# Eight raw weight buffers, a re-spaced split schedule and earlier token gathers in an attention + routed experts + FFN kernel

## The chip, the cores and the metric

The kernel runs on one core of one Trainium2 chip. The metric is the device time of one execution in microseconds (us); the number compared is the median of several executions. TensorE (PE) multiplies and transposes, VectorE (DVE) and ScalarE (ACT) do elementwise work, GpSimd (POOL) issues indirect gathers, and SyncE (SP) issues most DMAs.

## The reference

Three stages run one after the other on 1536 tokens of width 512, all in float32.

1. Chunked local attention with 8 memory keys per head; its output is x[1536, 512].
2. A routed layer with 8 experts: `expert = argmax(x @ w_gate)`, a softmax weight for the chosen expert, at most 384 tokens per expert, then `relu(x_e @ w1[e]) @ w2[e]` with w1[e] 512x1024 and w2[e] 1024x512.
3. A dense layer: `h = x @ w_in` (512x2048), `g = max(0.01 h, h)`, `g @ w_out` (2048x512). Its two weight matrices arrive as 64-bit floats.

```python
h = np.maximum(np.einsum('ecd,edf->ecf', disp, w1), 0.0)
y = np.einsum('ecf,efd->ecd', h, w2)
...
h = x @ w_in
g = np.maximum(0.01 * h, h)
return (g @ w_out).astype(np.float32)
```

## The kernel before

**Weights.** Every matmul is done as three fp32r matmuls on high and low parts (high times low, high times high, low times high), so each weight tile has to be split. A 512 KB piece (an item) is loaded by SP into a raw buffer (tile `raw`, `load_ahead`, L178 to L187); ACT casts its high part into a ring slot (L221) and DVE subtracts for the low part (L225). The subtraction frees the raw buffer, and only then SP may issue the next load: at most `RAWS` = 5 items are loaded or waiting. An expert has eight items (A0, B0, A1, B1 of two items each; A is w1, B is w2). The ring has eight slots, four per expert, and a slot is free once the expert two earlier has used it (`RETIRE`, `slot_free`).

The FFN's weights have 32 items of 64-bit floats. Their conversion, `wide_stages` (L122 to L148), has three stages: ACT writes a square into a scratch tile `c` and rescales the low word (L132, L133); DVE does six operations (L137 to L145); ACT and DVE split the result (L119, L120). An item passes one stage at a call, then the next one a call later, and the split two calls after that.

**Order.** The order of work on each engine is the program's order. `feed(n)` advances the weight generator by n items at hand-set places: after each of the six phases of an expert (`FEED_FIRST` for expert 0, `FEED_MID` for 1 to 5, `FEED_NEXT`, `FEED_LAST`), and after some steps of the FFN (`FEED_FFN`). `enter(e + 1)` at the end of expert e feeds what is still missing of the next expert's weights. Counted along this order, the items split at the ends of experts 0 to 5 are 20, 29, 38, 46, 54 and 62.

**An expert** (`expert`, L676 to L762). If it has more than 256 tokens, a third block of 128 rows is done first (`block`, under the `If` of L684): transposes (L771), `xc` split by ACT and DVE (L773, L774), 24 matmuls (L787), then relu, transposes and 24 more (L805). Then come six phases. Above 128 tokens, phases 0 to 3 compute hidden units (L694) and phases 2 to 5 the rows (L701); with 1 to 128 tokens the 24 matmuls of L706 fill phases 0 and 1, transposes (L711) phases 2 and 3, and L715 phases 4 and 5; with none, TensorE only fills (L719). After each of phases 0 to 3, ACT and DVE write the split hidden values `hs` (L742, L746) and for phases 0 and 1 a plain copy `t` (L745). Inside the phases named by `NEXT_AT`, the next expert's tokens are transposed on TensorE (L660, into the single PSUM buffer `tp`) and split by ACT and DVE into `xsT` (L662, L663). At the end DVE copies y[0] and ACT y[1] to `o` (L760), and SP stores them.

In this input the experts differ: 0, 5 and 6 have up to 128 tokens, 1 has up to 256, 2, 3 and 7 have the third block, 4 has no tokens.

**Gathers.** POOL gathers 128 token rows at a time into one of five `nat` buffers (L640), three per expert (`gathers`, nested in `experts`), issued in program order at the start of the expert before.

Of the kernel before, what the change touches and what calls it, by code (L numbers as in the profile page):

```python
# [6 lines left out]
F32 = mybir.dt.float32  # L7
# [11 lines left out]
P = 128  # L19
# [10 lines left out]
NEG = -1e30  # L30
RING = 8
NQ = 4
RAWS = 5
FLIGHT = 3
SHARE = (0,)
GAP_FEED = 2
# [1 line left out]
DRAIN_FEED = ((0, 0), (1, 0), (1, 0), (0, 0))  # L38
ROUTE_STEPS = 5
ROUTE_FEED = ((15, 0), (19, 0), (20, 0))  # L40
FEED_FIRST = (2, 1, 1, 3, 2, 3)
FEED_MID = (2, 0, 0, 3, 2, 2)
FEED_NEXT = (2, 0, 0, 1, 1, 0)
FEED_LAST = (1, 1, 1, 1, 0, 0)
FEED_GAP = 2
RETIRE = (None, ("A", 0), None, ("A", 1), ("B", 0), ("B", 1))
FEED_FFN = (0, 2, 3, 4, 6, 7, 8, 10, 11)
NEXT_AT = (2, 3)
MIN_HIGH = 2.0 ** -15 * 1.125


class Builder:
# [69 lines left out]
    def wide_stages(self, raw, dst, eng):  # L122
        nc, dv = self.nc, self.nc.vector
        w = raw.rearrange("p (n w) -> p n w", w=2)
        lo_w, lo_f, hi_f = w[:, :, 0], w[:, :, 0].bitcast(F32), w[:, :, 1].bitcast(F32)

        def buf(tag):
            return self.mp.tile([P, 512], U32, name=tag, tag=tag, bufs=3)

        c = [buf("c0")]  # L130
        cf = [c[0].bitcast(F32)]
        nc.scalar.activation(out=cf[0], in_=hi_f, func=AF.Square)  # L132
        nc.scalar.activation(out=lo_f, in_=lo_w, func=AF.Copy, scale=2.0 ** -52)  # L133
        yield
        c.append(buf("c1"))
        cf.append(c[1].bitcast(F32))
        dv.scalar_tensor_tensor(out=cf[0], in0=cf[0], scalar=MIN_HIGH * MIN_HIGH, in1=hi_f,  # L137
                                op0=ALU.is_ge, op1=ALU.mult)
        dv.tensor_scalar(out=c[1], in0=c[0], scalar1=3, scalar2=0x3FFFFFFF,  # L139
                         op0=ALU.logical_shift_left, op1=ALU.bitwise_and)  # L140
        dv.scalar_tensor_tensor(out=c[1], in0=c[0], scalar=0xC0000000, in1=c[1],  # L141
                                op0=ALU.bitwise_and, op1=ALU.bitwise_or)
        dv.tensor_scalar(out=c[0], in0=c[1], scalar1=0xFF800000, scalar2=None, op0=ALU.bitwise_and)  # L143
        dv.tensor_tensor(out=cf[0], in0=lo_f, in1=cf[0], op=ALU.mult)  # L144
        dv.tensor_tensor(out=cf[1], in0=cf[1], in1=cf[0], op=ALU.add)  # L145
        self.held -= 1
        yield
        self.split_piece(cf[1], dst, eng)  # L148

# [26 lines left out]
        return src[m * P:(m + 2) * P].rearrange("(k p) f -> p k f", p=P)  # L176

    def load_ahead(self):  # L178
        while self.held < RAWS:
            nxt = next(self.rawgen, None)  # L180
            if nxt is None:
                return
            raw = self.spool.tile([P, 1024], F32 if nxt[1] < E else U32, name="raw", tag="raw", bufs=RAWS)
            self.nc.sync.dma_start(out=raw.rearrange("p (k f) -> p k f", k=2) if nxt[1] < E else raw,
                                   in_=self.weight_source(*nxt))
            self.raws.append(raw)
            self.held += 1  # L187

    def weights_gen(self):
        flying, count = [], 0  # L190

        def advance():
            for rec in list(flying):
                rec[1] += 1
                if rec[1] == 1 or rec[1] == rec[2]:
                    next(rec[0], None)
                    if rec[1] > 1:
                        flying.remove(rec)
                        self.ready.add(rec[3])

        for kind, e, i, m in self.items:
            self.load_ahead()
            if m == 0:
                while e == E and i > self.quarter or (kind, e, i) not in self.W and not self.slot_free():
                    advance()
                    yield
                self.weight_slot((kind, e, i))
            raw, dst = self.raws.pop(0), self.W[(kind, e, i)]
            if e == E:
                advance()  # L210
                st = self.wide_stages(raw, (dst[:, 0, m, :], dst[:, 1, m, :]),
                                      self.nc.vector)
                next(st)
                flying.append([st, 0, self.flight, (kind, e, i, m)])
                yield
                continue
            advance()
            count += 1
            raw = raw.rearrange("p (k f) -> p k f", k=2)
            hi, lo = dst[:, 0, m:m + 2, :], dst[:, 1, m:m + 2, :]  # L220
            self.nc.scalar.copy(out=hi, in_=raw)  # L221
            mode = self.share[count % len(self.share)]
            for j, n in ((0, 2),) if mode == 0 else ((0, 1), (1, 1)):
                eng = self.nc.gpsimd if (mode == 2 or mode == 1 and j) else self.nc.vector
                eng.tensor_tensor(out=lo[:, j:j + n], in0=raw[:, j:j + n], in1=hi[:, j:j + n].bitcast(F32),  # L225
                                  op=ALU.subtract)
            self.ready |= {(kind, e, i, m), (kind, e, i, m + 1)}
            self.held -= 1
            self.load_ahead()
            yield  # L230
        while flying:
            advance()
            yield
# [293 lines left out]
    def prologue(self):  # L527
        nc = self.nc
        with ExitStack() as ctx:
# [46 lines left out]
            ones_cols(self.vb[2])  # L576
            self.load_qk(3)
            NU = 2 * NI
            self.W, self.ready, self.raws, self.held, self.items = {}, set(), [], 0, self.weight_items()
            self.rawgen = iter(self.items)  # L580
            self.wgen = self.weights_gen()
            self.flight, self.share, self.quarter = FLIGHT, SHARE, 0
            for u in range(NU + 4):
# [54 lines left out]
    def gather(self, idx, col, src):  # L638
# [2 lines left out]
                                          in_offset=bass.IndirectOffsetOnAxis(ap=idx[:, col:col + 1], axis=0))  # L641
        return t

    def clear_rows(self, e):
        for j in range(2, self.nj):
            r0 = e * self.slots + j * P
            self.nc.sync.dma_start(out=self.ys[r0:r0 + P, :].rearrange("p (r d) -> p r d", d=P),
                                   in_=self.zero.unsqueeze(1).to_broadcast([P, DM // P, P]))
# [27 lines left out]
    def expert(self, e):  # L676
        nc, nj = self.nc, self.nj
        xs = self.xsT.pop(e)
        feeds = {0: FEED_FIRST, E - 2: FEED_NEXT, E - 1: FEED_LAST}.get(e, FEED_MID)
        pcnt = self.pcnts.pop(e)  # L680
        if nj > 2:
            cnt, nat = self.cnts.pop(e), self.natx.pop(e, [])
# [44 lines left out]
        for ph, (many, few) in enumerate(phases):  # L727
            if ph < 4:
                hps[ph] = self.mps.tile([P, 512], F32, name="h", tag="h", bufs=3)
            with self.tc.If(pcnt > P) as cmp:  # L730
                many()
            with cmp.Else():
                if ph == 5:
                    fill(y[1])
                with self.tc.If(pcnt > 0) as some:
                    few()
                with some.Else():
                    if ph != 4:
                        fill(hps[ph] if ph < 4 else y[0])
            if ph < 4:  # L740
                h = hs[ph] = self.mp.tile([P, 2, 512], F32R, name="hs", tag="hg", bufs=4)
                nc.scalar.activation(out=h[:, 0, :], in_=hps[ph], func=AF.Relu)  # L742
                if ph < 2:
                    ts[ph] = self.mp.tile([P, 512], F32, name="t", tag="hg", bufs=4)
                    nc.scalar.activation(out=ts[ph], in_=hps[ph], func=AF.Relu)  # L745
                nc.vector.scalar_tensor_tensor(out=h[:, 1, :], in0=hps[ph], scalar=0.0,  # L746
                                               in1=h[:, 0, :].bitcast(F32), op0=ALU.max, op1=ALU.subtract)
            self.retired |= {RETIRE[ph] and (RETIRE[ph][0], e, RETIRE[ph][1])}
            if e + 1 < E:
                if ph == 0:  # L750
                    self.clear_rows(e + 1)
                    self.counts(e + 1)
                if ph in NEXT_AT:
                    self.expert_x(e + 1, NEXT_AT.index(ph))
            self.feed(feeds[ph])
        if e + 1 < E:
            self.enter(e + 1)
        for j in range(2):
            o = self.npool.tile([P, DM], F32, name="o", tag="o", bufs=2)
            (nc.scalar.copy if j else nc.vector.tensor_copy)(out=o, in_=y[j])  # L760
            r0 = e * self.slots + j * P
            (nc.scalar if e == E - 1 and j else nc.sync).dma_start(out=self.ys[r0:r0 + P, :], in_=o)  # L762

    def block(self, e, j, nat):
        nc = self.nc
# [56 lines left out]
    def experts(self):  # L822
        nc = self.nc
        self.nat, self.natx, self.xsT, self.cnts, self.pcnts = {}, {}, {}, {}, {}

        def gathers(e):
            self.nat[e] = [self.gather(self.tab, e * self.nj + j, self.xs) for j in range(2)]
            self.natx[e] = [self.gather(self.tab, e * self.nj + 2, self.xs)] if self.nj == 3 else []

        gathers(0)  # L830
        self.feed(GAP_FEED)
        self.keep_warm(self.mps.tile([P, 512], F32, name="tp", tag="acc", bufs=4), WARM[1])
        self.expert_x(0, 0)
        self.expert_x(0, 1, "acc", 4)
        self.enter(0)
        self.counts(0)
        for e in range(E):
            if e + 1 < E:
                gathers(e + 1)
            self.expert(e)  # L840


# [112 lines left out]
    def build(self):  # L955
# [11 lines left out]
        self.prologue()  # L967
        with ExitStack() as c2:
            self.mp = self.npool = self.pool(c2, "moe")
            self.mps = self.pool(c2, "mps", space=PSUM)  # L970
            self.experts()
            self.ffn()
# [35 lines left out]
```

## Time and profile before

| what | value |
|---|---|
| runs (us) | 623.01 (median), 623.58, 619.49 |
| profiled execution | 626.9 us, span 625.1 us |
| TensorE busy | 548.3 us (88% of the span) |
| VectorE busy | 408.2 us (65%) |
| ScalarE busy | 300.4 us (48%) |
| mean granted TensorE clock | 0.945 of full speed |

The span runs from the first to the last instruction of the profiled execution; the execution's time is 1.8 us longer. In the rows below times are us from the start of the span. Attention and routing take the first 96 us, the experts 96 to 330, the FFN the rest. A row of a timeline is a run of like instructions on one engine; what stands in brackets is the idle time just before it and what ended it.

### The profile page before, as it was taken

The numbers are of one execution on the slowest core, as the hardware profiler recorded it, in microseconds if no ns is written. First come the engines' busy times: TensorE is split into PE (matmuls) and PEld (weight loads), VectorE is DVE, ScalarE is ACT, GpSimd is POOL, SyncE is SP. The second block draws the span as 40 slices with busy tenths as digits, with TensorE's granted clock in tenths as the row PEclk, the third lists the DMA queues.
The fourth block names the chain that finished last, engine by engine and source line by source line (L and its number), as shares of the span: only waits on it lengthen the run. The fifth ranks groups of instructions, "written<-read, shape, count | busy, mean of one in ns | idle before, by whom it ended". The sixth has DMA issues, their size and how long they took to land.

```text
span 625.1 us, 9434 instructions
## 1 busy us (share of the span) xinstructions
PE 548.3 (88%) x3393; PEld 446.0 (71%) x3393; DVE 408.2 (65%) x672; ACT 300.4 (48%) x520; POOL 69.0 (11%) x104
## 2 busy tenths in 40 slices
PE   7799946796996993688997899999999999999997
PEld 6566635685895982466886778788887788777886
DVE  4776776836136347676298687874888878885443
ACT  7999646635135346465243455545344344432211
POOL 7323242101001012000004110000000000000000
PEclk9999967789898996698999999999999999999999
DMA  7899949966328139975136331310222211000111
GB/s 187 188 213 195 283 145 333 332 213 220 134 70 288 66 103 331 297 225 221 60 100 222 100 118 35 100 50 21 68 68 67 69 57 44 1 1 0 68 67 68
DMA packets 66857, 84.80 MB, mean 136 GB/s; under 512 B 22768, under 2 KB 39408, under 8 KB 66800
## 3 DMA queue, kind: packets, MB, share of 16 engines
q1 hardware_dynamic: 61456, 68.95, 36.5%
q0 software_dynamic: 3904, 12.59, 6.7%
q10 hardware_dynamic: 1440, 2.49, 1.1%
q8 instruction: 38, 0.62, 0.4%
q14 instruction: 19, 0.16, 0.1%
HBM read 70.64 MB, written 13.37 MB: 134 GB/s over the span
## 4 chain that ended last, share of the span: by engine, by line
DVE 25%; PE 23%; ACT 5%; issue 3%; DMA 1%; DVEq 0%; ACTq 0%; POOL 0%; POOLq 0%
PE acc L914 9%; PE h L893 9%; DVE t L902 3%; DVE gt L904 3%; ACT gt L903 3%; DVE c L144 3%; DVE c L141 3%; DVE c L137 2%; DVE ring L120 2%; DVE c L139 2%; DVE c L143 2%; DVE c L145 1%; PE h L706 1%; DVE total L930 1%; PE acc L715 1%
## 5 line engine op out<-in xcount | busy, mean ns | idle before, releaser
L893 PE MATMUL h<-x,ring 128*128 128x512 f32 (+1 forms) x600 | 141.8, 386 | 3.1 <-ACT x L878 2.7
L914 PE MATMUL acc<-ring,gt 128*128 128x512 f32 x576 | 138.7, 390 | 4.6 <-DVE rest L930 2.9
L914 PEld LDWEIGHTS acc<-ring,gt 128*128 128x128 f32 x576 | 107.7, 188 | 28.9 <-ACT t L901 5.0
L893 PEld LDWEIGHTS h<-x,ring 128*128 128x128 f32 x600 | 110.1, 191 | 25.3 <-ACT x L878 3.6
L225 DVE TENSOR_TENSOR ring<-raw,ring 128x1024 fp32r<-128x1024 f32 x64 | 75.5, 1223 | 15.6 <-ACT ring L221 14.6
L903 ACT CAST gt<-t 128x512 fp32r<-128x512 f32 x48 | 29.8, 621 | 96.1 <-DVE t L902 96.1
L221 ACT CAST ring<-raw 128x1024 fp32r<-128x1024 f32 x64 | 63.9, 1052 | 17.6 <-DMA raw<-in_moe_w_dram 17.6
L901 ACT COPY t<-h 128x512 f32<-128x512 f32 x48 | 28.2, 587 | 63.2 <-PE h L893 63.1
L902 DVE SCALAR_TENSOR_TENSOR t<-h,t 128x512 f32<-128x512 f32 x48 | 32.9, 685 | 35.4 <-ACT t L901 35.4
L904 DVE TENSOR_TENSOR gt<-t,gt 128x512 fp32r<-128x512 f32 x48 | 33.3, 693 | 33.0 <-ACT gt L903 33.0
L746 DVE SCALAR_TENSOR_TENSOR hs<-h,hs 128x512 fp32r<-128x512 f32 x32 | 21.7, 687 | 49.6 <-ACT hs L742 26.9
L694 PE MATMUL h<-xsT,ring 128*128 128x256 f32 x384 | 49.4, 289 | 3.7 <-issue 3.1
L694 PEld LDWEIGHTS h<-xsT,ring 128*128 128x128 f32 x384 | 48.4, 197 | 4.6 <-issue 4.3
L742 ACT ACTIVATE hs<-h 128x512 fp32r<-128x512 f32 x32 | 19.5, 608 | 58.7 <-PE acc L701 34.8
L701 PE MATMUL acc<-ring,hs 128*128 128x512 f32 x192 | 46.0, 392 | 0.0
L640 POOL DMA_INDIRECT nat<-xs,tab x24 | 24.1, 1006 | 159.5 <-PE tp L660 137.9
L701 PEld LDWEIGHTS acc<-ring,hs 128*128 128x128 f32 x192 | 35.3, 188 | 7.0
L787 PE MATMUL h<-ring,xc 128*128 128x512 f32 x72 | 22.4, 470 | 11.0 <-ACT xc L773 11.0
L706 PE MATMUL h<-ring,xsT 128*128 128x512 f32 x72 | 24.3, 509 | 8.3 <-DVEq L684 5.5
L706 PEld LDWEIGHTS h<-ring,xsT 128*128 128x128 f32 x72 | 18.0, 257 | 14.5 <-issue 7.5
L787 PEld LDWEIGHTS h<-ring,xc 128*128 128x128 f32 x72 | 16.2, 233 | 15.3 <-ACT xc L773 11.7
L144 DVE TENSOR_TENSOR c<-raw,c 128x512 f32<-128x512 f32 x32 | 22.2, 693 | 1.2
(162 smaller groups left out, 739.1 us busy)
## 6 DMA issues: line engine op xcount, KB each, us to landing
raw<-in_moe_w_dram SPq DMA_DIRECT2D x64, 512.0 KB, 5.6
raw<-in_moe_w_in_dram SPq DMA_DIRECT2D x16, 512.0 KB, 3.8
raw<-in_moe_w_out_dram SPq DMA_DIRECT2D x16, 512.0 KB, 3.4
ys<-o SPq DMA_DIRECT2D x15, 256.0 KB, 6.0
kn<-in_k_dram SPq DMA_DIRECT2D x16, 192.0 KB, 2.7
qn<-in_q_dram SPq DMA_DIRECT2D x16, 192.0 KB, 4.1
xs<-x POOLq DMA_DIRECT2D x16, 192.0 KB, 4.6
vb<-in_v_dram SPq DMA_DIRECT2D x12, 176.0 KB
```

What stands on the lines that cost most here:

```text
L144: dv.tensor_tensor(out=cf[0], in0=lo_f, in1=cf[0], op=ALU.mult)
L221: self.nc.scalar.copy(out=hi, in_=raw)
L225: eng.tensor_tensor(out=lo[:, j:j + n], in0=raw[:, j:j + n], in1=hi[:, j:j + n].bitcast(F32), op=ALU.subtract)
L694: nc.tensor.matmul(hps[f // 2][:, f % 2 * 256:f % 2 * 256 + 256], w["A", f // 4][:, wi, k, c], xs[xi][:, k, :], start=(n == 0), stop=(n == ...
L701: nc.tensor.matmul(y[j], hs[f // 2][:, hi, c:c + P], w["B", f // 4][:, wi, f % 4, :], start=(f == 0 and n == 0), stop=(f == 7 and n == 2))
L706: nc.tensor.matmul(hps[i], xs[xi][:, k, :P], w["A", i][:, wi, k, :], start=(n == 0), stop=(n == 11))
L787: nc.tensor.matmul(hp[i], xc[:, xi, k, :], w[:, wi, k, :], start=(n == 0), stop=(n == 11))
L893: nc.tensor.matmul(hps[s][:, t], w[:, wi, k, c], X[g][:, xi, k, t], start=(n == 0), stop=(n == 11))
L902: nc.vector.scalar_tensor_tensor(out=t, in0=hp, scalar=0.01, in1=t, op0=ALU.mult, op1=ALU.max)
L903: nc.scalar.copy(out=gt[:, 0, :], in_=t)
L904: nc.vector.tensor_tensor(out=gt[:, 1, :], in0=t, in1=gt[:, 0, :].bitcast(F32), op=ALU.subtract)
L914: nc.tensor.matmul(acc[g][i], gt[:, hi, i * P:(i + 1) * P], w[:, wi, f, :], start=(f == 0 and n == 0), stop=(f == HQ - 1 and n == 2))
```

## The change

Two parts touch the weights, two the tokens, two are small.

- The scratch of the 64-bit conversion was six 2 KB tiles per partition (`c0`, `c1`, three buffers each). It becomes three 4 KB tiles of the tag `more`, each with both halves. While expert weights are loaded, these three also serve as raw buffers (`home` 1), so eight items can be loaded or waiting. FFN items still use the five old ones only.
- The feed counts become a table per expert. Counted the same way, the items split at the ends of experts 0 to 5 become 16, 27, 38, 46, 53 and 61 (a feed that meets a slot not yet free does nothing, before and after).
- Gathers of expert e + 2 are issued in phase 3 of expert e; those of experts 0 and 1 before the first expert.
- The next expert's tokens are transposed in phases 0 and 2 instead of 2 and 3.
- The plain copy `t` goes ahead of `hs` on ACT.
- The last expert's y[0] is stored from ACT's queue instead of SP's.

```diff
-RAWS = 5
+RAWS, MORE = 5, 3
-FEED_FIRST = (2, 1, 1, 3, 2, 3)
-FEED_MID = (2, 0, 0, 3, 2, 2)
-FEED_NEXT = (2, 0, 0, 1, 1, 0)
-FEED_LAST = (1, 1, 1, 1, 0, 0)
+FEED = ((2, 0, 0, 3, 2, 1), (3, 0, 0, 3, 3, 2), (3, 0, 0, 3, 3, 2), (2, 0, 0, 3, 3, 1),
+        (2, 0, 0, 3, 2, 1), (2, 0, 0, 3, 2, 1), (2, 0, 0, 1, 1, 0), (1, 1, 1, 1, 0, 0))
-NEXT_AT = (2, 3)
+NEXT_AT = (0, 2)
...
-        c = [buf("c0")]
+        both = self.mp.tile([P, 2, 512], U32, name="c", tag="more", bufs=MORE)
+        c = [both[:, i] for i in range(2)]
...
-        self.held -= 1
+        self.room[0] += 1
...
     def load_ahead(self):
-        while self.held < RAWS:
-            nxt = next(self.rawgen, None)
-            if nxt is None:
+        while self.rawnext is not None:
+            narrow = self.rawnext[1] < E
+            home = 0 if self.room[0] else 1
+            if not self.room[home] or home and not narrow:
                 return
-            raw = self.spool.tile([P, 1024], F32 if nxt[1] < E else U32, name="raw", tag="raw", bufs=RAWS)
+            nxt, self.rawnext = self.rawnext, next(self.rawgen, None)
+            self.room[home] -= 1
+            if home:
+                raw = self.mp.tile([P, 1024], F32, name="more", tag="more", bufs=MORE)
+            else:
+                raw = self.spool.tile([P, 1024], F32 if narrow else U32, name="raw", tag="raw", bufs=RAWS)
...
+    def gathers(self, e):
+        nat = [self.gather(self.tab, e * self.nj + j, self.xs) for j in range(min(self.nj, 3))]
+        self.nat[e], self.natx[e] = nat[:2], nat[2:] if self.nj == 3 else []
...
-                nc.scalar.activation(out=h[:, 0, :], in_=hps[ph], func=AF.Relu)
                 if ph < 2:
                     ts[ph] = self.mp.tile([P, 512], F32, name="t", tag="hg", bufs=4)
                     nc.scalar.activation(out=ts[ph], in_=hps[ph], func=AF.Relu)
+                nc.scalar.activation(out=h[:, 0, :], in_=hps[ph], func=AF.Relu)
...
+                if ph == 3 and e + 2 < E:
+                    self.gathers(e + 2)
-            self.feed(feeds[ph])
+            self.feed(FEED[e][ph])
...
-            (nc.scalar if e == E - 1 and j else nc.sync).dma_start(out=self.ys[r0:r0 + P, :], in_=o)
+            (nc.scalar if e == E - 1 else nc.sync).dma_start(out=self.ys[r0:r0 + P, :], in_=o)
...
+        self.gathers(1)
         for e in range(E):
-            if e + 1 < E:
-                gathers(e + 1)
             self.expert(e)
...
             self.mp = self.npool = self.pool(c2, "moe")
+            self.room[1] = MORE
```

## Rows read from the trace of the kernel before

**Rows 1.** Busy time by stretch: expert 4, FFN from 414, from 447.

```profile
core 0: us, PE busy (x) PEld busy (x) DVE busy (x) ACT busy (x) POOL busy (x), PEclk, DMA share, GB/s
...
236.10:250.30 14.20, 5.48 (x14) 3.18 (x15) 9.87 (x12) 9.47 (x15) 2.54 (x3) 0.60 0.98 333
...
414.00:447.00 33.00, 33.00 (x147) 27.33 (x146) 21.56 (x36) 15.16 (x26) 0.00 (x0) 1.00 0.18 57
447.00:563.00 116.00, 112.30 (x492) 91.73 (x490) 97.59 (x160) 46.74 (x81) 0.00 (x0) 1.00 0.14 43
```

**Rows 2.** TensorE's timeline, experts 0 to 7: start, length, line, idle before and releaser.

```profile
110.44 1.12 PE L660 MATMUL tp<-ident,nat 128*128 128x128 f32 x4 [2.74 <-DVE xsT L663]
111.20 5.23 PE L715 MATMUL acc<-ring,hs 128*128 128x512 f32 x12
...
126.18 7.49 PE L694 MATMUL h<-xsT,ring 128*128 128x256 f32 x48 [3.06 <-issue]
...
142.68 5.74 PE L701 MATMUL acc<-ring,hs 128*128 128x512 f32 x24
...
154.31 7.45 PE L787 MATMUL h<-ring,xc 128*128 128x512 f32 x19 [5.46 <-ACT xc L773]
...
169.11 8.80 PE L694 MATMUL h<-xsT,ring 128*128 128x256 f32 x72
...
198.10 6.11 PE L787 MATMUL h<-ring,xc 128*128 128x512 f32 x19 [5.01 <-ACT xc L773]
...
261.28 5.28 PE L706 MATMUL h<-ring,xsT 128*128 128x512 f32 x12 [5.51 <-DVEq L684]
...
295.22 4.61 PE L787 MATMUL h<-ring,xc 128*128 128x512 f32 x19 [0.52 <-ACT xc L773]
```

**Rows 3.** ACT's timeline, end of expert 1 and start of expert 2.

```profile
143.48 4.85 ACT L221 CAST ring<-raw 128x1024 fp32r<-128x1024 f32 x5
151.04 1.04 ACT L221 CAST ring<-raw 128x1024 fp32r<-128x1024 f32 x1 [2.71 <-DMA raw<-in_moe_w_dram]
...
153.88 0.65 ACT L773 CAST xc<-tp 128x256 fp32r<-128x256 f32 x2
```

**Rows 4.** DVE's timeline, ends of experts 0 and 3, inside and at the end of 4.

```profile
113.15 4.63 DVE L225 TENSOR_TENSOR ring<-raw,ring 128x1024 fp32r<-128x1024 f32 x4 [0.25 <-ACT ring L221]
...
125.23 0.68 DVE L760 COPY o<-acc 128x512 f32<-128x512 f32 x1
...
238.35 1.22 DVE L225 TENSOR_TENSOR ring<-raw,ring 128x1024 fp32r<-128x1024 f32 x1 [1.31 <-ACT ring L221]
...
248.39 0.69 DVE L663 TENSOR_TENSOR xsT<-tp,xsT 128x512 fp32r<-128x512 f32 x1 [1.23 <-ACT xsT L662]
...
259.25 1.23 DVE L225 TENSOR_TENSOR ring<-raw,ring 128x1024 fp32r<-128x1024 f32 x1 [4.15 <-ACT ring L221]
```

**Rows 5.** Waits, 96 to 330: who waited for whom, total, times, longest.

```profile
ACT ring L221 <- DMA raw<-in_moe_w_dram: 17.6, 11, 5.0
...
PE tp L660 <- DVE xsT L663: 8.9, 4, 3.3
```

**Rows 6.** DMA by stretch (columns as in rows 1): experts 0 and 1.

```profile
106.00:110.00 4.00, 1.20 (x9) 0.73 (x7) 4.00 (x6) 4.00 (x8) 0.00 (x0) 0.90 1.00 347
...
136.00:142.00 6.00, 6.00 (x41) 5.47 (x40) 1.29 (x2) 1.08 (x2) 0.00 (x0) 1.00 0.02 6
```

**Rows 7.** One FFN step with a feed: ACT's rescaling, DVE's split and last stage-two operation.

```profile
475.63 0.67 ACT L132 ACTIVATE c<-raw 128x512 f32<-128x512 f32 x1
...
475.84 0.68 DVE L120 TENSOR_TENSOR ring<-c,ring 128x512 fp32r<-128x512 f32 x1
...
479.54 0.69 DVE L145 TENSOR_TENSOR c<-c,c 128x512 f32<-128x512 f32 x1
```

**Rows 8.** The hand-over to the FFN: ACT's store of y[1], the first gather.

```profile
330.47 0.33 ACTq L762 DMA_DIRECT2D ys<-o  x1
...
334.45 0.95 POOL L640 DMA_INDIRECT nat<-ys,yidx  x1 [63.03 <-issue]
```

More of the change, by code (lines that the diff above doesn't have):

```diff
@@ L125, in wide_stages @@
         lo_w, lo_f, hi_f = w[:, :, 0], w[:, :, 0].bitcast(F32), w[:, :, 1].bitcast(F32)
-        def buf(tag):
-            return self.mp.tile([P, 512], U32, name=tag, tag=tag, bufs=3)
-        c = [buf("c0")]
-        cf = [c[0].bitcast(F32)]
+        both = self.mp.tile([P, 2, 512], U32, name="c", tag="more", bufs=MORE)
+        c = [both[:, i] for i in range(2)]
+        cf = [t.bitcast(F32) for t in c]
         nc.scalar.activation(out=cf[0], in_=hi_f, func=AF.Square)
@@ L134, in wide_stages @@
         yield
-        c.append(buf("c1"))
-        cf.append(c[1].bitcast(F32))
         dv.scalar_tensor_tensor(out=cf[0], in0=cf[0], scalar=MIN_HIGH * MIN_HIGH, in1=hi_f,
@@ L178, in load_ahead @@
     def load_ahead(self):
-        while self.held < RAWS:
-            nxt = next(self.rawgen, None)
-            if nxt is None:
+        while self.rawnext is not None:
+            narrow = self.rawnext[1] < E
+            home = 0 if self.room[0] else 1
+            if not self.room[home] or home and not narrow:
                 return
-            raw = self.spool.tile([P, 1024], F32 if nxt[1] < E else U32, name="raw", tag="raw", bufs=RAWS)
-            self.nc.sync.dma_start(out=raw.rearrange("p (k f) -> p k f", k=2) if nxt[1] < E else raw,
+            nxt, self.rawnext = self.rawnext, next(self.rawgen, None)
[4 more added lines that the diff above has]
+                raw = self.spool.tile([P, 1024], F32 if narrow else U32, name="raw", tag="raw", bufs=RAWS)
+            self.nc.sync.dma_start(out=raw.rearrange("p (k f) -> p k f", k=2) if narrow else raw,
                                    in_=self.weight_source(*nxt))
-            self.raws.append(raw)
-            self.held += 1
+            self.raws.append((raw, home))
     def weights_gen(self):
@@ L207, in weights_gen @@
                 self.weight_slot((kind, e, i))
-            raw, dst = self.raws.pop(0), self.W[(kind, e, i)]
+            (raw, home), dst = self.raws.pop(0), self.W[(kind, e, i)]
             if e == E:
@@ L227, in weights_gen @@
             self.ready |= {(kind, e, i, m), (kind, e, i, m + 1)}
-            self.held -= 1
+            self.room[home] += 1
             self.load_ahead()
@@ L578, in prologue @@
             NU = 2 * NI
-            self.W, self.ready, self.raws, self.held, self.items = {}, set(), [], 0, self.weight_items()
+            self.W, self.ready, self.raws, self.items = {}, set(), [], self.weight_items()
+            self.room = [RAWS, 0]
             self.rawgen = iter(self.items)
+            self.rawnext = next(self.rawgen)
             self.wgen = self.weights_gen()
@@ L678, in expert @@
         xs = self.xsT.pop(e)
-        feeds = {0: FEED_FIRST, E - 2: FEED_NEXT, E - 1: FEED_LAST}.get(e, FEED_MID)
         pcnt = self.pcnts.pop(e)
@@ L824, in experts @@
         self.nat, self.natx, self.xsT, self.cnts, self.pcnts = {}, {}, {}, {}, {}
[L826 to L830, printed above, removed]
+        self.gathers(0)
         self.feed(GAP_FEED)
```

## Prediction

> **What bounds the kernel now.** I read the windows by stretch first, then the three timelines, the waits, and the DMA by stretch. The FFN from 414 on is TensorE at its pace: 33.0 us busy of 33.0, then 112.3 of 116 with DVE at 97.6 close behind [rows 1]. The loss is among the experts. Expert 4 has no tokens and still takes 14.2 us at a granted clock of 0.60 [rows 1]. TensorE's timeline shows the others [rows 2]. Its holes sit where one expert follows another: 3.06 us before expert 1's phase 1, 5.46 and 5.01 us before the third blocks of experts 2 and 3, 5.51 us before expert 5's phase 1. The block of expert 7, with no split batch of narrow weights ahead of it, waits 0.52 us [rows 2].
>
> Two things make these holes. First, the split batch of phases 3 to 5 stands ahead of the end-of-expert copies in ACT's and DVE's order, and it runs out of raw buffers: ACT waits 17.6 us for weight DMAs, eleven times, at most 5.0 us [rows 5]; in expert 1 it stood still 2.71 us before the sixth split and reached `xc` only at 153.88 [rows 3]. Second, TensorE cannot go past phase 0 of an expert before DVE has passed the `If` of L684, because the skipped block still takes its turn in the PSUM tag `h`. The row at 261.28 names DVE at L684 as releaser [rows 2]; the row at 126.18 says only "issue", but comes 0.27 us after DVE's last copy of expert 0 (125.23 plus 0.68) [rows 4], and I read it the same way. After a hole TensorE runs slow: 19 matmuls take 7.45 and 6.11 us after the long holes, 4.61 after the short one [rows 2].
>
> **Part by part.** Splits cost DVE 1.16 us each in a batch (4.63 for four) [rows 4] and ACT 0.97 (4.85 for five) [rows 3].
>
> *Expert 0 into 1.* Four of its twelve splits go (20 items at its end become 16). DVE's last batch began at 113.15 [rows 4]; the splits of phases 1 and 2 no longer stand ahead of it, 2 x 1.16, so it begins near 110.8, and holds six: 7.0, plus the copy 0.68, is 118.5. TensorE followed 0.27 later and would at 118.8, against 126.18: 7.4. TensorE itself gets there: without the stall of 2.74 its rows start at 108.4; 2.9 + 0.3 + 2.9 for them and 2.9 for expert 1's phase 0 (a third of 8.80) end at 117.4 at full speed, 119.8 if the first twelve stay at 5.23 [rows 2]. The 48 matmuls after it took 7.49 where 48 of a run of 72 take 5.87 [rows 2]: another 1.6. **Gain 9.0**, bounds 6 and 9.
>
> *Expert 1 into 2.* Its last batch holds eight splits, one more than before (27 items at its end, 19 of them before phase 3), but no DMA wait: the eight raw buffers were filled during the phases before, when the DMA engines stood nearly idle (0.02 from 136 to 142) [rows 6]. ACT's batch began at 143.48 [rows 3], 4.94 before TensorE's rows ended at 148.42 [rows 2]; with the `xsT` cast moved to phase 2 it begins 0.5 earlier. Eight times 0.97 end 2.3 after the rows, the copy and the two halves of `xc` 1.3 later, so the block starts 3.7 after the rows instead of 5.9: a hole of 3.3 instead of 5.46. I price the 19 matmuls at 6.11, the row after the nearer hole, not 4.61: that is 9.4 against 12.9. DVE's eight splits, copy and `xc` end 6.3 after the rows, when the first eight of the 19 are through, so the low parts come just in time. **Gain 3.5**, bounds 2.2 (7.45 stays) and 5.0.
>
> *Expert 2 into 3.* The same hole and price against 5.01 + 6.11: **gain 1.7**, bounds 0.4 and 3.2.
>
> *Expert 3 into 4.* Both schedules split six items in phases 3 to 5 (each loses one feed to an unfree slot). DVE's idle 1.31 before the last [rows 4] goes, and the `xsT` operation ahead of the batch, 0.6: **gain 1.9**, bounds 0.6 and 1.9.
>
> *Expert 4*, a chain through DVE alone. The DMA wait of 4.15, the wait of 1.23 for the second token half, since half a transposition now comes in phase 0, and one split of 1.16 go [rows 4]: **gain 6.5**, bounds 2.4 (the DMA is full here, 0.98 [rows 1]) and 6.5.
>
> *Experts 5 and 6.* `tp` is a single buffer; TensorE waited for it 8.9 us in four places, 3.3 the longest [rows 5], and 2.74 is expert 0's [rows 2]. Phases 0 and 2 lie apart, so the other 2.9 go. DVE's queue is next in line and keeps their ends where its splits put them. **Gain 2.8**, bounds 0 and 5.
>
> *What should cost nothing.* The gathers: POOL has its own order and each waits only for its buffer, so issuing them earlier in the program moves none; the earlier transposes free buffers sooner. `t` ahead of `hs`: half a microsecond between two ACT operations, and DVE waited for the later of both. One FFN item comes later, 4.3 us of DVE at the end of the FFN's first quarter, hidden by the stretch from 414 where DVE is busy 21.6 of 33 [rows 1]; uncovered it costs 4.3.
>
> *The shared scratch pair.* The square of item n + 3 (ACT) now waits for DVE's L120 of item n. Behind it in ACT's queue stands the next step's copy `t`, for which DVE waits. DVE does L120 at 475.84, and its stage-two operations end at 480.2 [rows 7]: square, rescaling (0.67 each) and `t` fit into those 3.7 us. I take 0, below nothing since it only adds a wait; the upper end is the second rival.
>
> *The hand-over.* Both stores of expert 7 now go through ACT, where y[1]'s copy stands behind y[0]'s, its 0.68 copy and one issue of 0.33. The first gather, at 334.45, waits for both [rows 8]. **Loss 0.9**, bounds 0 and 1.2.
>
> *Three loads further ahead in expert 0.* From 106 to 110 the DMA engines are full (1.00, 347 GB/s) [rows 6]: a load of 0.52 MB takes 1.5 us of them. The token gathers of expert 1 are needed near 103. I take 0, since POOL starts them before most of the added loads; the ends are 0 and three loads, 4.5. The Trainium skill (DMA: Bandwidth & Descriptors, Issuing engines are not separate DMA queues) says that transfers from any engine run on the same 16 DMA engines and interleave; by that rule the added loads would delay the gathers, and the sum would be up to 4.5 smaller. The full stretches agree with it; no row shows a gather's own delay.
>
> Sum: 9.0 + 3.5 + 1.7 + 1.9 + 6.5 + 2.8 - 0.9 = 24.5. From the profiled 626.9 that is 602.4. That execution lies 3.9 above the median of 623.0, so against the median I say **598.5**.
>
> **The rivals.**
>
> *Contention takes the early gains.* The DMA engines are full in expert 0 and again in expert 4. If raw loads and gathers hold each other up there, the waits move instead of going: expert 0 keeps only its 2.74 and the boundary half of its 7.4, some 5 in place of 9.0, expert 4 its lower bound of 2.4, and the blocks their 2.2 and 0.4. With 0.6, 2.8 and the loss that is 12.5, or 610.5. For it: the full rows. Against: by the counts each batch needs only items whose buffers were freed a whole batch earlier.
>
> *The scratch pair holds ACT, slower.* If the square is released only when DVE is through with the six operations behind L120, then square, rescaling and `t`, about 1.9 us, follow each of them on DVE's path. The FFN starts 24 more items, so 24 x 1.9 = 46 at most, less the 11 that DVE has spare from 414 to 447 [rows 1]: 35, or 633.5 with the gains. It decides as soon as the release comes more than 1.8 us after L120. Against: L120 is ahead of the six in DVE's order.
>
> *The edit does little.* If the holes are DVE's queue alone, a batch of eight ends where seven with a wait ended, and only the transposition stalls and the hand-over are left: 8.9 - 0.9, with half of them lost to the `If`, 4: 619.
>
> *More comes back.* The clock holds through the shorter holes: 1.5 in each of two blocks (6.11 against 4.61), 2.4 in expert 5 (5.28 against 2.9), 2.2 more in experts 5 and 6 up to their bound: 591.
>
> **How the numbers follow.** Forecast 0.58, contention 0.21, more 0.09, little 0.07, slower 0.05. The forecast's own range, with the unknown costs, is 592 to 605. Eight in ten are held by 589 to 613, which takes in the contention case and the larger gain; little and slower lie outside. About 1% (6 us) is what a measurement here can tell from none: faster by more has the forecast, contention and more, 0.88 and a little of the fourth, together 0.89; within 1% 0.06; slower 0.05.
>
> **What would show it.** Right: ACT's waits for weight DMAs fall from 17.6 to under 4; the hole before expert 1's phase 1 is under 1 us; the holes before the blocks of experts 2 and 3 are near 3.3; expert 4 lasts some 8 us less between DVE's copies; no stall at L660 over 0.5; the FFN's length is unchanged within 2. Wrong: ACT's square waits for DVE beyond L120, TensorE waits for a gather in expert 0, or the holes keep their length with DVE's splits as releaser.

## The result and the profile after

The changed kernel takes 602.57 us (median of four, 602.11 to 604.45), the kernel before in the same session 621.75 (619.49 to 623.58): ratio 0.970, 95% interval [0.966, 0.974]. The forecast was 598.5, range 589 to 613. The profiled execution after is 602.32 us with a span of 600.6; the one before was 626.9 with 625.1.

TensorE's timeline after, experts 0 to 5 (start, length, line, matmuls, idle before and releaser). Line numbers moved: L793 answers to L787 of before, L698 to L694, L710 to L706, L665 to L660, L688 to L684, L779 and L780 to L773 and L774, L766 to L760:

```profile
97.63 5.46 PE L710 MATMUL h<-ring,xsT 128*128 128x512 f32 x12 [1.44 <-DMA nat<-xs,tab]
102.88 0.85 PE L665 MATMUL tp<-ident,nat 128*128 128x128 f32 x4
...
118.19 0.63 PE L665 MATMUL tp<-ident,nat 128*128 128x128 f32 x4 [0.34 <-DVEq L688]
118.57 5.99 PE L698 MATMUL h<-xsT,ring 128*128 128x256 f32 x48
...
142.37 2.11 PE L793 MATMUL h<-ring,xc 128*128 128x512 f32 x8 [3.13 <-ACT xc L779]
145.43 2.83 PE L793 MATMUL h<-ring,xc 128*128 128x512 f32 x11 [0.94 <-DVE xc L780]
...
182.67 7.42 PE L793 MATMUL h<-ring,xc 128*128 128x512 f32 x19 [3.13 <-ACT xc L779]
...
224.94 0.63 PE L665 MATMUL tp<-ident,nat 128*128 128x128 f32 x4 [2.57 <-DVEq L688]
...
240.05 3.03 PE L710 MATMUL h<-ring,xsT 128*128 128x512 f32 x12
```

The hole of 3.06 us in expert 1 [rows 2] is 0.34, the two block holes of 5.46 and 5.01 are 3.13 each, the hole of 5.51 in expert 5 is gone and its twelve matmuls run at full speed, 3.03 in place of 5.28. ACT's batch at the end of expert 1 runs through, eight casts from two kinds of buffer (compare [rows 3]):

```profile
133.89 1.99 ACT L220 CAST ring<-more 128x1024 fp32r<-128x1024 f32 x2
135.78 4.84 ACT L220 CAST ring<-raw 128x1024 fp32r<-128x1024 f32 x5
140.52 1.05 ACT L220 CAST ring<-more 128x1024 fp32r<-128x1024 f32 x1
141.47 0.59 ACT L766 COPY o<-acc 128x512 f32<-128x512 f32 x1
141.94 0.65 ACT L779 CAST xc<-tp 128x256 fp32r<-128x256 f32 x2
```

Among the waits of the expert stage, ACT's for weight DMAs, 17.6 us before [rows 5], no longer appears. DVE's copies into and out of expert 4 are 13.7 us apart instead of 20.9, and the window of that expert shows the DMA engines as full as before (0.99) with DVE busy 12.38 of 13.8:

```profile
223.95 0.68 DVE L766 COPY o<-acc 128x512 f32<-128x512 f32 x1
...
237.69 0.68 DVE L766 COPY o<-acc 128x512 f32<-128x512 f32 x1
```

```profile
220.40:234.20 13.80, 6.05 (x17) 2.85 (x16) 12.38 (x15) 11.31 (x17) 3.49 (x4) 0.71 0.99 330
```

Two stretches got longer: the hand-over and the FFN. ACT's queue with both stores of expert 7, then POOL's first gather (compare [rows 8]):

```profile
302.70 0.33 ACTq L768 DMA_DIRECT2D ys<-o  x1
303.13 0.58 ACT L766 COPY o<-acc 128x512 f32<-128x512 f32 x1 [3.46 <-DVE o L766]
303.74 0.33 ACTq L768 DMA_DIRECT2D ys<-o  x1
```

```profile
307.74 0.95 POOL L641 DMA_INDIRECT nat<-ys,yidx  x1 [62.26 <-issue]
```

### The profile page after: what moved, and what is told of

Its sections match the earlier page's. It is cut to its first block, busy times and chain, and to the rows that moved or that the text cites. A ratio compares the mean times of both kernels' runs of the same rounds, so it can differ in the third digit from the quotient of the medians.

```text
span 600.6 us, 9423 instructions
## 1 busy us (share of the span) xinstructions
PE 538.5 (90%) x3393; PEld 437.6 (73%) x3393; DVE 406.5 (68%) x672; ACT 299.5 (50%) x520; POOL 71.5 (12%) x104
## 4 chain that ended last, share of the span: by engine, by line
DVE 29%; PE 18%; ACT 6%; issue 3%; DMA 1%; ACTq 0%; DVEq 0%; POOL 0%; POOLq 0%
PE acc L915 7%; PE h L894 6%; DVE t L903 4%; DVE gt L905 4%; ACT gt L904 4%; DVE c L138 3%; DVE c L135 3%; DVE c L131 3%; DVE ring L118 2%; DVE c L133 2%; DVE c L137 2%; DVE total L931 2%; DVE c L139 1%; PE h L793 1%; PE acc L719 1%
## 5 line engine op out<-in xcount | busy, mean ns | idle before, releaser
L224 DVE TENSOR_TENSOR ring<-raw,ring 128x1024 fp32r<-128x1024 f32 x43 | 50.8, 1221 | 1.8 <-ACT ring L220 0.5
L698 PE MATMUL h<-xsT,ring 128*128 128x256 f32 x384 | 48.3, 284 | 0.6 <-ACT ring L220 0.6
L698 PEld LDWEIGHTS h<-xsT,ring 128*128 128x128 f32 x384 | 47.0, 191 | 1.3 <-ACT ring L220 1.0
L220 ACT CAST ring<-raw 128x1024 fp32r<-128x1024 f32 x43 | 43.2, 1065 | 0.0
L641 POOL DMA_INDIRECT nat<-xs,tab x24 | 25.7, 1071 | 132.3 <-PE tp L665 92.7
L128 ACT ACTIVATE c<-raw 128x512 f32<-128x512 f32 x32 | 21.8, 681 | 22.3 <-DVE ring L118 22.3
L793 PE MATMUL h<-ring,xc 128*128 128x512 f32 x72 | 21.2, 448 | 7.7 <-ACT xc L779 6.8
L710 PE MATMUL h<-ring,xsT 128*128 128x512 f32 x72 | 22.9, 479 | 3.0 <-DMA nat<-xs,tab 1.4
L224 DVE TENSOR_TENSOR ring<-more,ring 128x1024 fp32r<-128x1024 f32 x21 | 24.6, 1219 | 0.4 <-ACT ring L220 0.2
L793 PEld LDWEIGHTS h<-ring,xc 128*128 128x128 f32 x72 | 15.0, 217 | 12.1 <-ACT xc L779 7.5
```

The lines of the kernel that those rows point to most:

```text
L641: self.nc.gpsimd.indirect_dma_start(out=t, out_offset=None, in_=src, in_offset=bass.IndirectOffsetOnAxis(ap=idx[:, col:col + 1], axis=0))
L698: nc.tensor.matmul(hps[f // 2][:, f % 2 * 256:f % 2 * 256 + 256], w["A", f // 4][:, wi, k, c], xs[xi][:, k, :], start=(n == 0), stop=(n == ...
L793: nc.tensor.matmul(hp[i], xc[:, xi, k, :], w[:, wi, k, :], start=(n == 0), stop=(n == 11))
```

## The experiments

All kernels in one table. A stage is read from that kernel's own profiled execution, which can lie some us off the median in the second column (old_feeds' is 3.1 above): the experts from the first L706 matmul to the warm-up matmuls after expert 7, the hand-over from there to the first dense matmul, the FFN to the end of the span. Ratios are to the kernel before on the same chip; its medians there were 622.56 for the four runs from before_again to next_only, 621.99 for after_again, sp_store, scratch4 and spread, and 622.64 for five_raws, old_feeds, old_next and spread3_sp.

| kernel | us | ratio, interval | experts | hand-over | FFN |
|---|---|---|---|---|---|
| before (first profile) | 621.75 | 1 | 231.8 | 11.6 | 283.9 |
| before_again | 621.08 | 0.998 [0.994, 1.001] | 223.3 | 11.6 | 283.9 |
| after | 602.57 | 0.970 [0.966, 0.974] | 204.1 | 13.6 | 285.3 |
| after_again | 601.70 | 0.968 [0.963, 0.973] | 204.0 | 13.5 | 285.5 |
| buffers_only | 606.31 | 0.973 [0.969, 0.978] | 212.6 | 11.6 | 283.9 |
| feeds_only | 616.02 | 0.987 [0.983, 0.992] | 220.1 | 11.8 | 285.2 |
| next_only | 619.45 | 0.997 [0.994, 1.000] | 225.1 | 11.9 | 284.3 |
| five_raws | 616.22 | 0.991 [0.987, 0.994] | 219.5 | 13.8 | 285.1 |
| old_feeds | 606.27 | 0.974 [0.970, 0.978] | 211.3 | 13.2 | 283.2 |
| old_next | 609.53 | 0.979 [0.974, 0.983] | 212.2 | 13.3 | 285.0 |
| sp_store | 599.98 | 0.965 [0.960, 0.970] | 203.8 | 12.2 | 285.7 |
| scratch4 | 602.90 | 0.969 [0.964, 0.974] | 204.7 | 13.8 | 285.3 |
| spread | 593.95 | 0.956 [0.951, 0.960] | 198.8 | 13.6 | 284.5 |
| spread3_sp | 589.87 | 0.948 [0.944, 0.952] | 193.8 | 11.8 | 285.3 |

**A second profile of before** (no edit).

> The kernel before, once more, for a second profile. Theory A: the profiled execution of before (626.9 us, 5 us above the median of its runs) was a dear draw of the expert stage, where half-speed stretches follow the holes: a new profile lies at 619 to 624, with its expert stage (first L706 matmul to the transposes that open expert 7, 196.2 us before) 3 to 6 us shorter, and the FFN the same within 0.5. Theory B: the profile itself costs before some 5 us: the new profiled execution is again 625 to 628 with the same stages, and the gain that two profiles show is overstated by it.

The new profiled execution is 616.9 us, the fastest of its ten. Hand-over and FFN agree to 0.1 us, the experts are 8.5 us shorter and the stretch ahead of them 1.5. Theory A holds, by more than it said: 616.9 lies below its range. Of the 8.5, 3.7 are in expert 4: its two DVE copies are 17.2 us apart here, 20.9 in the first profile,

```profile
236.38 0.68 DVE L760 COPY o<-acc 128x512 f32<-128x512 f32 x1
253.57 0.68 DVE L760 COPY o<-acc 128x512 f32<-128x512 f32 x1
```

and ACT's wait for its last weight load is 1.11 us in place of 5.0.

```profile
251.34 1.05 ACT L221 CAST ring<-raw 128x1024 fp32r<-128x1024 f32 x1 [1.11 <-DMA raw<-in_moe_w_dram]
```

**The raw buffers alone.**

```diff
+RAWS, MORE = 5, 3
...
+            self.room[1] = MORE
```

The cut shows two lines. The scratch pairs and the place of the gathers in the program are also as in the changed kernel; the feed counts, the phases, the order of `t` and `hs` and the store of y[0] are as before.

> The kernel before with the three extra raw buffers (and the shared scratch) alone; feeds, transposition phases, order of the copies and store as before. Main theory (the gain has three sources: raw buffers that end ACT's waits for weight DMAs in experts 1 to 5, four splits fewer in expert 0, earlier transposes): expert 0 keeps its twelve splits on a full DMA, so about 8 us faster, 613, with holes before the blocks of experts 2 and 3 near 3.5 and expert 0 to 1 little changed. Rival F (the feeds do it): under 2 us, 620 or more. Rival B (the buffers do it): 16 us or more, 606 or less.

It took 606.31, 16 us off: twice my theory, and at the edge of rival B. The block holes fell to 2.18, shorter than the 3.13 of the changed kernel: the batch is seven here and eight there (old_feeds, with seven, has 2.18 and 2.19; old_next, with eight, 3.14 twice). The hole in expert 1 stayed. The gathers' place is part of this run, but the traces give it no share: in both kernels each gather among the experts starts when TensorE has used its buffer or passed the `If`, and TensorE waits for none after expert 0's.

```profile
123.72 5.99 PE L698 MATMUL h<-xsT,ring 128*128 128x256 f32 x48 [2.79 <-issue]
...
147.07 2.11 PE L793 MATMUL h<-ring,xc 128*128 128x512 f32 x8 [2.18 <-ACT xc L779]
149.94 2.80 PE L793 MATMUL h<-ring,xc 128*128 128x512 f32 x11 [0.77 <-DVE xc L780]
```

**The feeds alone.**

```diff
-FEED_FIRST = (2, 1, 1, 3, 2, 3)
...
+FEED = ((2, 0, 0, 3, 2, 1), (3, 0, 0, 3, 3, 2), (3, 0, 0, 3, 3, 2), (2, 0, 0, 3, 3, 1),
...
```

> The kernel before with the new feed table alone, five raw buffers. Main theory: expert 0 into 1 gains 6 to 9, but the batches of eight in experts 1 and 2 run out of raw buffers and wait longer there, so 3 to 6 us in all, about 617. Rival F: 12 us or more, 610 or less. Rival B: within 2 us of before.

616.02: 6.5 us by the medians, some 8 by the ratio of 0.987, a little above my 3 to 6 and short of rival F. As the theory had it, the blocks of experts 2 and 3 wait longer than before, 6.18 and 6.08 us (L784 is the block's line in this kernel), and expert 1's hole is gone.

```profile
147.87 7.46 PE L784 MATMUL h<-ring,xc 128*128 128x512 f32 x19 [6.18 <-ACT xc L770]
```

**The transposition phases alone.**

```diff
-NEXT_AT = (2, 3)
+NEXT_AT = (0, 2)
```

> The kernel before with the next expert's tokens transposed in phases 0 and 2 instead of 2 and 3, nothing else. Main theory: TensorE's 8.9 us of stalls for the single transposition buffer go, but in experts 4 and 5 DVE's queue sets the end anyway: 3 to 6 us faster, about 617. Rivals F and B: within 2 us of before, as the DMA waits that follow take the room.

The interval takes in no change (0.3%, some 2 us, by the ratio); I had said 3 to 6 us. The stall of 2.74 in expert 0 went, and came back as a longer wait in expert 1, now in front of the transposes:

```profile
125.15 1.09 PE L660 MATMUL tp<-ident,nat 128*128 128x128 f32 x4 [7.34 <-DVEq L684]
```

The transposition buffer `tp` is used by the skipped block as well, so in phase 0 the transposes stand behind DVE's passage of the `If`, as the hidden units of phase 1 did. This place, where TensorE cannot go on until DVE has passed the `If`, is called the gate below.

**Each of the three taken out of the change.**

```diff
-            self.room[1] = MORE
...
-FEED = ((2, 0, 0, 3, 2, 1), (3, 0, 0, 3, 3, 2), (3, 0, 0, 3, 3, 2), (2, 0, 0, 3, 3, 1),
+FEED = ((2, 1, 1, 3, 2, 3), (2, 0, 0, 3, 2, 2), (2, 0, 0, 3, 2, 2), (2, 0, 0, 3, 2, 2),
...
-NEXT_AT = (0, 2)
+NEXT_AT = (2, 3)
```

These are three edits of three kernels: five_raws, old_feeds (the old counts again) and old_next. The order of `t` and `hs` and the store through ACT stay as changed in all three.

> The changed kernel without the three extra raw buffers (the scratch is still three pairs); feeds, phases and stores as changed. The extra buffers alone gave 2.7%, the feeds alone 1.3%, the phases alone 0.3%, together 4.2 where the whole change gives 3.1, so they overlap. Theory (the buffers take away the waits of ACT for weight DMAs in every batch, which the feeds and phases only shift): back to 613 to 616, with holes of 5 to 6 before the blocks of experts 2 and 3. Rival (any one of them is enough): 607 or less.

> The changed kernel with the old feed counts: eight raw buffers, transposes in phases 0 and 2. Theory: expert 0's twelve splits sit in front of the gate of L688 again, so the hole there comes back (4 us or more), but the batches of experts 1 and 2 are one split shorter (holes of 2.2 instead of 3.1, as with the buffers alone): 604 to 606, 2 to 4 us slower than the changed kernel. Rival (the feed table is worth what it gave alone, 1.3%): 609 or more.

> The changed kernel with the transposes in phases 2 and 3 again. Theory: once the splits no longer hold DVE back, the single transposition buffer is the wait that is left in experts 0, 4, 5 and 6 (some 9 us of stalls on TensorE before): 606 to 609, 4 to 7 us slower than the changed kernel, though the phases alone gave only 2 to 3. Rival (their worth is the same wherever they stand): 603 to 605.

All three came out just past the upper end of the theory's range and short of the rivals' values. Without the buffers 616.22: ACT waits 18.1 us for weight DMAs, as before the change, and both block holes are over 6 us. Without the feeds 606.27, as with the buffers alone: the early transposes then stand 6.31 us at the gate. Without the early phases 609.53: the stalls at `tp` are back. First the waits of five_raws, then its TensorE, then TensorE of old_feeds, then of old_next:

```profile
ACT ring L220 <- DMA raw<-in_moe_w_dram: 18.1, 12, 5.2
```

```profile
149.46 6.81 PE L793 MATMUL h<-ring,xc 128*128 128x512 f32 x19 [6.67 <-ACT xc L779]
...
254.68 1.09 PE L665 MATMUL tp<-ident,nat 128*128 128x128 f32 x4 [5.12 <-DVEq L688]
```

```profile
127.25 1.09 PE L665 MATMUL tp<-ident,nat 128*128 128x128 f32 x4 [6.31 <-DVEq L688]
```

```profile
110.17 0.66 PE L665 MATMUL tp<-ident,nat 128*128 128x128 f32 x4 [1.87 <-DVE xsT L668]
...
235.00 1.12 PE L665 MATMUL tp<-ident,nat 128*128 128x128 f32 x4 [3.32 <-DVE xsT L668]
```

So the parts are not a sum. Buffers are worth 16 us alone and 13 to 14 on top of the rest; phases some 2 alone, which is not clear of nothing, nothing measurable on top of the buffers (there the hand-over through ACT, 13.2 against 11.6, hides some 1.6), and 6 to 7 with buffers and feeds. The feeds need the early phases as well: old_next has buffers and feeds, and its experts take 212.2 where the buffers alone give 212.6; with the early phases they take 204.1.

**The changed kernel as base for the next three** (no edit).

> The changed kernel as it is, as the base for the three that share its chip. Both theories: 602 to 603, some 19 us below before.

601.70, just under the 602 to 603 expected; six executions from 600.3 to 605.5. ACT waits once for a weight load, 0.9 us.

**Storing y[0] through SP.**

```diff
-            (nc.scalar if e == E - 1 else nc.sync).dma_start(...)
+            (nc.scalar if e == E - 1 and j else nc.sync).dma_start(...)
```

> The changed kernel with expert 7's y[0] stored from SP's queue again. From the last row matmul of expert 7 to the first transpose of the FFN took 8.6 us before and 10.6 after. Theory: ACT's order causes it (the copy of y[1] waits for y[0]'s store): 1 to 2 us faster than the changed kernel, the stretch back at 8.6 to 9.3. Rival (the gathers of the FFN meet weight loads on the DMA engines): same time within 0.5 us, the stretch stays above 10.

599.98 against 601.70; the intervals of the two ratios overlap, so the time alone does not decide. The trace does: ACT copies y[1] at once, the first gather starts 4.8 us after the rows end (at 300.77) instead of 6.1, the first transpose 9.0 after instead of 10.6. ACT's order accounts for the 1.3 us of the first gather. The edit also moves SP's next weight loads behind the store, from 0.3 us before the rows end to 1.5 after, so a share of these loads in the rest is not excluded.

```profile
300.97 0.59 ACT L766 COPY o<-acc 128x512 f32<-128x512 f32 x1 [2.24 <-PE acc L705]
301.58 0.33 ACTq L768 DMA_DIRECT2D ys<-o  x1
```

```profile
305.54 0.95 POOL L641 DMA_INDIRECT nat<-ys,yidx  x1 [60.92 <-DMA ys<-o]
```

In the table the hand-over is 13.2 to 13.8 in the seven profiles of kernels that store through ACT alone and 11.6 to 12.2 in all others.

**No wait for the scratch pair.**

```diff
-RAWS, MORE = 5, 3
+RAWS, MORE = 4, 4
```

> The changed kernel with four old raw buffers and four scratch pairs (still eight in all), so that the square of an FFN item no longer waits for the split of the item three before. Theory (the FFN's 1.4 us, 278.0 before and 279.4 after from the first dense matmul to the last sum, come from the one item that is converted later): within 1 us of the changed kernel, ACT's wait on L118 gone. Rival (the wait for the scratch pair holds ACT on the path): 1.5 us faster or more, the FFN back at 278.0.

In the changed kernel ACT waits 22.3 us for L118 of DVE, 23 times:

```profile
ACT c L128 <- DVE ring L118: 22.3, 23, 2.6
```

With four pairs that wait is gone and neither the time nor the FFN (285.3) moves. The edit also leaves the FFN's items four raw buffers in place of five, so alone it does not settle the point; buffers_only does, with the three shared pairs, five raw buffers and an FFN of 283.9, as before. The pair is off the path, as predicted. The FFN is 283.2 to 284.3 in the five profiles with the old counts and 285.0 to 285.7 in eight of the nine with a new table (spread has 284.5). All nine show one wait of TensorE for ACT's L929 (L925 in feeds_only), 0.97 to 1.00 us, and none of the five does. So the longer FFN goes with the table; that the one item converted later makes it is argued, not shown.

**The splits spread over the phases.**

```diff
-(3, 0, 0, 3, 3, 2), (3, 0, 0, 3, 3, 2)
+(3, 2, 1, 2, 2, 1), (3, 2, 1, 2, 2, 1)      experts 1 and 2
```

> The changed kernel with the splits of experts 1 and 2 spread over the phases: feeds 3, 2, 1, 2, 2, 1 instead of 3, 0, 0, 3, 3, 2, the same eleven. Theory (the batch of eight in phases 3 to 5 keeps ACT busy 3 us beyond the rows and DVE 6, and that leaves the holes of 3.13 before the blocks of experts 2 and 3 and the half-speed 7.42 in expert 3): holes under 1.2, both runs of 19 matmuls near 4.6, 4 to 8 us faster than the changed kernel. Rival (splits in phases 1 and 2 come in front of the hidden values and the token half, and only move the wait): within 1 us, with TensorE waiting for hs or xsT instead.

593.95, 7.8 us below the changed kernel. Both block holes are at the 0.52 of expert 7:

```profile
138.59 5.08 PE L793 MATMUL h<-ring,xc 128*128 128x512 f32 x19 [0.52 <-ACT xc L779]
...
175.47 4.62 PE L793 MATMUL h<-ring,xc 128*128 128x512 f32 x19 [0.52 <-ACT xc L779]
```

**Both, and expert 3 as well.**

```diff
-(2, 0, 0, 3, 3, 1)
+(2, 2, 0, 0, 3, 1)      expert 3, with the splits spread and y[0] through SP
```

> The spread feeds (594), expert 3's three feeds of phase 3 given as two in phase 1 (feeds 2, 2, 0, 0, 3, 1; one of the three met an unfree slot), and y[0] of expert 7 stored from SP's queue. Theory: SP's queue gives 1.7, expert 3's batch is two splits shorter at its end, so DVE passes the gate into expert 4 some 2.3 us earlier: 590 (588 to 592). Rival (expert 4's chain then waits for weight DMAs, as the loads are asked for at the same pace): 592 to 594, with ACT waiting for DMA in expert 4.

589.87, 0.948 [0.944, 0.952]: the fastest, some 12 us below the changed kernel. The gate into expert 4 holds the transposes 0.57 us, against 2.57 in the changed kernel and 3.69 in spread. The rival's wait is there but small: ACT waits for one weight load, 1.3 us.

```profile
212.75 0.63 PE L665 MATMUL tp<-ident,nat 128*128 128x128 f32 x4 [0.57 <-DVEq L688]
```

## Why the prediction was right, and where it was not

Step by step, in us gained: the profiled execution after against the first one before, and against the second (before_again):

| step | predicted | measured | against the second |
|---|---|---|---|
| expert 0 into 1, to the end of expert 1's 48 matmuls | 9.0 | 8.9 | 7.3 |
| to the end of the 19 matmuls of expert 2 | 3.5 | 4.4 | 4.2 |
| to the end of those of expert 3 | 1.7 | 0.6 | 0.8 |
| to DVE's copy at the end of expert 3 | 1.9 | 1.4 | 1.4 |
| to DVE's copy at the end of expert 4 | 6.5 | 7.2 | 3.5 |
| experts 5 and 6, to expert 7's first transposes | 2.8 | 5.3 | 2.1 |
| hand-over and the way to the first dense matmul | -0.9 | -2.0 | -2.0 |
| FFN | 0 | -1.5 | -1.5 |
| the start, ahead of the experts | 0 | 0.2 | -1.3 |
| sum | 24.5 | 24.5 | 14.5 |

The mechanism was right: the holes at the expert boundaries were ACT's DMA waits and DVE's late passage of the `If`, and they shrank where the queue sums said. Of the signs it named, ACT's waits for loads (none left), the hole in expert 1 (0.34), the block holes (3.13), expert 4 (7.2 shorter) and the FFN (1.5 longer) came out; one did not: the token transposes still stand 2.57 us in expert 4, at the gate and not at the buffer. That the sums agree to a tenth, and that the profile's own figure of 602.4 was met by 602.32, is luck: 2.5 us too little in experts 5 and 6 stands against 1.1 too much in expert 3, and 1.1 and 1.5 of loss that were left out at the hand-over and in the FFN, and the second profile of before gives the same steps 14.5.

**The step that failed is the last one**, "against the median I say 598.5". I took the profiled execution's 3.9 us above the median as an offset that stays. The second profile of before shows where such an excess sits. Of the 8.5 us by which its experts are shorter, 3.7 are expert 4, most of it ACT's wait for a load; another 3.8 are matmuls behind the gate, 5.99 in place of 7.49 for the 48 of expert 1 and 3.00 in place of 5.28 for twelve of expert 5. These waits and slow runs are what the change takes away. So the changed kernel loses that excess too, the gain against the median is 19 and not 24.5, and the time to state was the absolute 602.4. The forecast lay 4 us low for this reason, inside its range.

**Sizes.** Experts 5 and 6 were 2.5 too small: without the long hole expert 5's matmuls run at full speed, 3.03, a gain I had put among the rivals ("more comes back"). The two blocks came out at 5.0 together against 5.2, but that is luck again: I priced both at 6.11 for the 19 matmuls, and one took its first eight at full speed and the other 7.42 in all, most of it at half. The hand-over's loss was 1.1 too small and past its bound of 1.2: the first gather starts 1.3 us later after the rows and the transposes wait for it longer still, 4.18 for a gather. The FFN's loss, put at 0 because DVE's work for the later item would be covered, came as 1.5: TensorE waited 0.99 in the stretch that I had called cover,

```profile
402.79 3.01 PE L915 MATMUL acc<-ring,gt 128*128 128x512 f32 x12 [0.99 <-ACT rest L929]
```

and feeds_only, which has the table but not the scratch pair, has the same wait (1.00) and an FFN 1.3 longer.

**The rivals.** Contention fell: expert 0 kept its gain with the DMA engines full (1.08 from 98 to 102), and in expert 4, as full (0.99), ACT waits for no weight load. The Trainium skill (DMA: Bandwidth & Descriptors, Issuing engines are not separate DMA queues) says that transfers from all engines share the same 16 DMA engines and interleave; by that rule I had allowed up to 4.5 us for gathers delayed by the added loads. The transposes of expert 1's tokens at 102.88 started without idle time, so no such delay reached TensorE; whether the gathers themselves landed later is not shown. That the scratch pair holds ACT fell with scratch4 and buffers_only together. That the edit does little fell with the result. The order of `t` and `hs` and the place of the gathers in the program were not tried by themselves.

**What I had seen too simply.** The prediction gave each part its own gain. The experiments show one gate, DVE's arrival at the `If`, in series with the others: earlier transposes gain only once DVE arrives early, and the batches at the end of experts 1 and 2, which I took as given, cost the 7.8 us that spread got back.

## What to carry to other kernels

Where a profiled execution is longer than the median, ask in which stage the excess lies before you subtract a gain from the median: if the change removes the waits that vary, predict the absolute time, and take a second profile before you trust the size of a step (24.5 and 14.5 us here). With elementwise work queued in program order, the length of the batch ahead of a boundary sets the boundary: here more buffers paid 16 us, and spreading the batch another 8. Parts that stand at one gate do not add up: take each out of the whole as well as trying it alone. A buffer shared with a conditional block puts what uses it behind the slowest engine's passage of that condition, even when the block is skipped (7.34 and 6.31 us here).

## What the runs showed of the hardware

Executions of the kernel before went from 616.3 to 627.3 us, of the changed one from 600.3 to 605.5. In expert 4 of the kernel before, loads took 7.0 us to land in one profile (median of eight) and 5.8 in the other (of nine), and ACT's last wait for one was 5.0 and 1.11. That the wider spread comes from the five buffers is not shown: next_only has five too, and its ten executions lie between 617.6 and 621.9.

The same hole of 3.13 us left TensorE at either level of its clock. Ahead of both holes it ran without idle time at a granted clock of 1.00 (2.4 GHz). In the changed kernel's first profile expert 2's matmuls after it ran at 1.00 as well (2.11 for the first eight, 0.26 us each), and expert 3's 19 took 7.42, 0.39 each, at a granted clock of 0.50 (1.2 GHz) from 182.67 to 188.5; in its second profile it was the other way round, 7.29 for expert 2's 19 and 2.11 for expert 3's first eight. Why one and not the other was not settled.
